# Another order of the routing steps in the last batches, a relu placed between casts, and one drain of GpSimd

## The chip, the cores and the metric

The kernel runs on one core of a Trainium2 chip. TensorE (PE) multiplies matrices and transposes, with its results in PSUM; VectorE (DVE), ScalarE (ACT) and GpSimd (POOL) work on elements; SyncE (SP) issues most DMAs, GpSimd those that gather and scatter rows. Each engine takes its instructions in order. The metric is the device time of one execution in microseconds, as the median of several runs.

## The reference

Attention over 8 batches, 8 heads, 576 positions and 64 dimensions, in which a position sees the blocks of 64 up to its own, and then a mixture of 8 experts that sends each of the 4608 rows to one expert.

```
scores = where(mask, scale * q @ k.T, -1e9)
attn = exp(scores - max) / (sum + 1e-9)
x = (attn @ v).transpose(0, 2, 1, 3).reshape(4608, 512)
logits = x @ w_gate;  e_idx = argmax(logits)
gate_w = softmax(logits)[e_idx];  eom = sigmoid(x @ w_output_gate)
out[rows of e] = gate_w * eom[:, e] * (relu(x[rows] @ w1[e]) @ w2[e])
```

## The kernel before, in words

**Attention.** The 8 batches of 4 pairs of heads are 32 turns p of one pipeline; turn p computes scores and exponentials of pair p, the transposes of pair p-1 and the products with v of pair p-2. `PLAN` (line 310) is the written order of a turn. S0 to S4 are scores of the five row tiles, M0 to M4 their maxima and scalings (VectorE), E0A to E4 the exponentials (ScalarE), F0 to F6 transposes of the exponentials into PSUM, C0 to C6 the ScalarE copies that empty those buffers, V0, V1 and VM the products, X and XM their copies. "E4-" is E4 of the pair before. Between the second pair and the end of the last one, TensorE, VectorE and ScalarE keep this order as written (line 1154). Transposes, logits and other small results share a pool of three PSUM buffers, `ps_t`; scores have two, `ps_s`.

**A batch's finish.** At each "|" of the plan (eight in a turn) `turns()` advances every generator in `later` by one step. Once a batch's last product is done, `finish_batch` (line 508) joins them: `logits` multiplies x by the gate weights in two parts (lge for the last 64 rows, lgb for the others), `keep` copies them out (ke, kb), `turn_logits` and `turn_last` transpose them, `scale_logits` and `scale_last` divide by the softmax sums, `heads` adds over the heads, `choose` finds the expert as a one-hot `oh`, `ranks` and `own` count its place in the expert's list, `slots` gives the address, `shares`, `gather`, `gate` and `weights` give the row's factor, and `scatter` writes rows' numbers and factors to a table in DRAM with five GpSimd DMAs. T(t) and K(t) transpose and store the 128 rows of tile t. A batch's pace says how this is spread: over 32 steps (pace 1, four pairs) for batches 0 to 4, over 16 (pace 2, two pairs) for 5 and 6, and for batch 7 after all pairs with three steps to a turn. `heads` and two products of `choose` run on GpSimd for batches 0 to 5 and on VectorE for 6 and 7 (line 533).

**The end of attention.** After the last pair, `TAIL` runs out the pipeline, and `first_tiles` (line 1162) puts blocks of the first expert step's first layer between the turns of batch 7's finish, at the turns that `play` is given (line 1180). `route_rest` (line 742) then counts rows for each expert with one small matmul (line 688) and, by a chain of small VectorE operations, makes the list of the remaining steps: which weights (`wsel`, `wneed`) and which rows (`rti`) each takes.

**Expert steps.** A step takes 256, 128 or 64 rows of one expert. Rows are gathered by GpSimd, `turn_x` casts them (ScalarE) and subtracts (VectorE) to a high and a low 16-bit part and turns them by a DMA transpose; `stage_h` is the first layer with a relu after each half, `stage_y` the second, whose scaled result GpSimd scatters to the output (line 1057). Weights are fetched as 32-bit and split likewise (line 886). Steps 0 and 1 use the weights of one expert that is chosen early. From there, outside the turns, order on VectorE, ScalarE and GpSimd comes from the framework's scheduler. The last lines hold a branch for lists longer than 22 steps, which isn't taken here (line 1248).

Of the kernel before, what the change touches and what calls it, by code (L numbers as in the profile page):

```python
# [23 lines left out]
SYNC = mybir.DependencyInfo(mybir.DependencyClass.Sync, mybir.DependencyReason.DATA)  # L24
# [3 lines left out]
def block_attention_top1_moe(  # L28
# [11 lines left out]
    nc = tc.nc  # L40
    B, H, S, D = q.shape
# [253 lines left out]
    def constants():  # L295
# [12 lines left out]


    PLAN = """  # L310
        F0 S1 S0 M1 C0 | | E4- F1 C1 F2 M0 C2 E1A E1B E0A S2 E0B | F3 F4 C3 V0 S3 C4 |
        M2 F6 F5 E2A E2B M3 | C5 C6 V1 S4 VM | E3A E3B X M4 | | XM
    """.split()
    OPENING = "S1 S0 M1 M0 E1A E1B E0A E0B | S2 M2 E2A E2B S3 M3 E3A E3B | S4 M4 | | | E4".split()
    later = []
    CP = 1

    def turns():
        for g in list(later):
            if next(g, later) is later:  # L320
                later.remove(g)

    def play(plan, parts, at=()):

        r = 0
        for name in plan:
            if name != "|":
                parts.pop(name, lambda: None)()
                continue
            for i in range(at.count(r)):  # L330
                next(ahead, None)
            r += 1
            turns()
        while plan is TAIL and (later or r <= max(at, default=0)):
            for i in range(at.count(r)):
                next(ahead, None)
            r += 1
            turns()
# [168 lines left out]

    def finish_batch(b, sums, xT, pace):

        for i, fns in enumerate(finish_steps(b, sums, xT, pace)):  # L510
            for fn in fns:
                fn()
            if pace < 3 or i % pace == pace - 1:
                yield

    def finish_steps(b, sums, xT, pace):

# [12 lines left out]
        se = small.tile([P, NT], F32, name="se")  # L530
        sli = small.tile([P, NT], I32, name="sli")
        held = {}
        eng = nc.gpsimd if b < B - 2 else nc.vector

        def bank():
            return ps_t.tile([P, 512], F32, name="ps_t")
# [21 lines left out]
        def turn(t):  # L558
            r = ROWS[t]
            held["r", t] = pm = bank()  # L560
            for g in range(NP):
                nc.tensor.transpose(pm[0:r, P * g:P * g + P], xT[:, g, Q0[t]:Q0[t] + r], ident)

        def store(t):
            r = ROWS[t]
            xn = sb.tile([P, DM], F32, name="xn", bufs=4)
            nc.vector.tensor_tensor(
                xn[0:r].rearrange("p (h d) -> p h d", d=D), held["r", t][0:r].rearrange("p (h d) -> p h d", d=D),
                rec[0:r, t].unsqueeze(2).broadcast_to([r, H, D]), ALU.mult,
            )  # L570
            nc.sync.dma_start(x_d[b * S + Q0[t]:b * S + Q0[t] + r, :], xn[0:r])
# [98 lines left out]
        big, end = (0, 512), (512, S)  # L670
        T, K = (lambda t: lambda: turn(t)), (lambda t: lambda: store(t))
        lge, lgb, ke, kb = (partial(f, *c) for f in (logits, keep) for c in (end, big))
        if pace == 2:
            return [
                [lge, lgb], [ke], [kb, recips], [turn_logits, turn_last], [scale_logits, T(0)], [scale_last, heads, K(0)], [], [choose],
                [], [T(1), ranks], [own, K(1), T(2)], [K(2)], [slots, shares, T(3)], [gather, gate], [K(3), weights, scatter, T(4)], [K(4)],
            ]
        steps = [
            [lge], [ke, lgb], [kb, recips], [turn_logits], [scale_logits], [turn_last], [scale_last], [heads],
            [], [], [T(0)], [K(0)], [], [choose], [], [],  # L680
            [], [T(1), ranks], [own, K(1), T(2)], [K(2)], [T(3), slots], [shares], [K(3)], [],
            [], [], [T(4)], [K(4)], [gather], [gate], [weights, scatter], [],
        ]
        return steps if b < B - 1 else [fns for fns in steps if fns]

    def counts(col, name):
        pc = ps_t.tile([P, 512], F32, name="ps_t")
# [8 lines left out]
    first = const.tile([P, E], F32, name="first")  # L696
# [23 lines left out]
    def sequence(order, i0, used):  # L720
        seq = []
        for i, kind in enumerate(order):
            k = KINDS.index(kind)
            seq.append((BKIND[k] + used[k], KTILES[k], i0 + i))
            width[i0 + i] = KROWS[k] // KTILES[k]
            used[k] += 1
        return seq

    used = [0] * len(KINDS)
    steps = sequence(ORDER, 0, used)  # L730
# [183 lines left out]
    def split_all(fn, b, src):  # L914
        for c in range(4):
            fn(nc.vector, b, src[c], c)
# [35 lines left out]
    def stage_x(st, halves=None):  # L952
        c, n, i = st
        if i not in xs:
            xs[i] = (
                fs.tile([P, KD, n, P], F16, name="xh", padded_shape=[P, KD, 2, P]),
                fs.tile([P, KD, n, P], BF16, name="xl", padded_shape=[P, KD, 2, P]),
            )
        xh, xl = xs[i]
        for h in range(*(halves or (0, n))):  # L960
            other = i == 0 or (h and i > 1)
            px = (ps_t if other else ps_a).tile([P, 512], F32, name="ps_t" if other else "ps_a")
            px = px.rearrange("p (c n) -> p c n", c=KD)
            xv = xg[i % NXG][:, h].rearrange("t (c p) -> t c p", c=KD)
            for cc in range(KD):
                nc.tensor.transpose(px[:, cc, :], xv[:, cc, :], ident)
            act = nc.scalar.copy(xh[:, :, h], px)
            nc.vector.tensor_tensor(xl[:, :, h], px, xh[:, :, h], ALU.subtract)
        return act

    def turn_x(st, act=None):

        c, n, i = st
        xr = fb.tile([P, n, 2, DM], F16, name="xr", padded_shape=[P, 2, 2, DM], bufs=2)
        xt = fb.tile([P, n, 2, KD, P], F16, name="xt", padded_shape=[P, 2, 2, KD, P], bufs=TX + 1)
        for h in range(n):
            xv = xg[i % NXG][:, h]
            xh, xl = (xr[:, h, j] for j in range(2))
            with tc.issue_after(act.ins) if act else nullcontext():
                nc.scalar.copy(xh, xv)  # L980
            nc.vector.tensor_tensor(xl.bitcast(BF16), xv, xh, ALU.subtract)
        turned(xt.rearrange("p h a c n -> p (h a c) n"), xr.rearrange("t h a d -> t (h a d)"))
        xs[i] = xt[:, :, 0].rearrange("p h c n -> p c h n"), xt[:, :, 1].bitcast(BF16).rearrange("p h c n -> p c h n")

    def turned(dst, src):
        with chain():
            chained[0] = nc.sync.dma_start_transpose(dst, src)

    def stage_h(*args, **kw):
        for act in h_steps(*args, **kw):  # L990
            pay()
        return act

    def pay():
        while owed:
            owed.pop()()
# [134 lines left out]
    TAIL = None  # L1131
    for p in range(B * NP):
        b, hp = divmod(p, NP)
        u = p // 2
        h0 = units[u][1]
        if hp == 0:
            sums = small.tile([P, LAST * H + NP], F32, name="sums", bufs=3)
            xT = sb.tile([P, NP, S], F32, name="xT")
# [36 lines left out]
    TAIL = list(PLAN)  # L1175
    advance(TAIL, B * NP, {})
    advance(TAIL, B * NP + 1, {}, (0, 1))
    with tc.manual_schedule(engines={PE}):
        TAIL = []
        play(TAIL, {}, (1, 2, 3, 3, 3))  # L1180
    route_rest()
    for r in ahead:
        pass
# [1 line left out]
    first_ids = read[0].ins  # L1185
    fetch_x(steps[1], (1, 2))
    stage_y(steps[0])
    act = stage_x(steps[1], (1, 2))
    stage_y(steps[1], (0, 1))


# [11 lines left out]
    def split_after(act, fn, src, st):  # L1203

        with tc.issue_after(act.ins):
            split_all(fn, buf(st[2]), src)

    def run(seq, i0):

        n = len(seq)  # L1210
        for i in range(i0, n):
            if i + LI < n:
                fetch_ids(seq[i + LI])
            if i + LX < n:
                fetch_x(seq[i + LX])
            if i + 1 < n:
                fetch_w(seq[i + 1])

            def between(act):
                if i + TX < n:  # L1220
                    turn_x(seq[i + TX], act)
                if i + 1 < n:
                    split_after(act, split_w1, w1f, seq[i + 1])

            act = stage_h(seq[i], between=between)
            if i > i0:
                act = stage_y(seq[i - 1])
            if i + 1 < n:
                split_after(act, split_w2, w2f, seq[i + 1])
        stage_y(seq[n - 1])  # L1230
        pay()
# [6 lines left out]
    for i in range(3 + LX, 2 + LI):  # L1238
        fetch_ids(steps[i])

    turn_x(steps[2], act)
    turn_x(steps[3], act)
    act = stage_h(steps[1], (1, 2))
    split_after(act, split_w1, w1f, steps[2])
    act = stage_y(steps[1], (1, 2))
    split_after(act, split_w2, w2f, steps[2])
    run(steps, 2)
    mv = nc.values_load(more[0:1, 0:1], min_val=0, max_val=NSTEP)  # L1248
    with tc.If(mv > FKIND[1]):
        chained[0] = read[0] = None  # L1250
        for i in range(LI):
            fetch_ids(extra[i])
        for i in range(LX):
            fetch_x(extra[i])
        fetch_w(extra[0])
        split_all(split_w1, buf(extra[0][2]), w1f)
        split_all(split_w2, buf(extra[0][2]), w2f)
        for i in range(TX):
            turn_x(extra[i])
        run(extra, 0)  # L1260
# [30 lines left out]
```

## Time and profile before

| | |
|---|---|
| median of 3 runs | 769.02 us (767.86 to 769.62) |
| the profiled execution | 767.89 us, span 766.0 us |
| busy: TensorE, ScalarE, VectorE, GpSimd | 723.5, 533.0, 522.0, 344.6 us |
| mean granted clock of TensorE | 0.993 |

The span runs from the first to the last instruction. A timeline row gives start, duration, engine, line and operation, and in brackets how long the engine stood idle before it and what it waited for. Attention takes the first 361 us or so, its end and batch 7's finish some 20 more, the expert steps the rest.

### The profile page before, as it was taken

The page shows a single profiled execution, that of the slowest core. Times are in us where ns is not written, and L with a number is a line of the kernel's source. Part 1 is how long each engine was busy: PE and PEld are TensorE (multiplying, and loading weights), DVE is VectorE, ACT ScalarE, POOL GpSimd, SP SyncE. Part 2 cuts the span into 40 slices and gives each one's busy share as a digit, 9 for nine tenths or more (in the row PEclk, how much of TensorE's full clock was granted, in tenths as well). Part 3 has the DMA queues.
Part 4 walks back from the last instruction along what each step waited for, and adds up shares of the span by engine and source line. Part 5 has one row for each costly group of instructions (what it writes and reads, how often), then busy time and mean ns, then how long its engine had stood idle before and what let it go on. Part 6 is the DMA issues. An engine that isn't in the chain of part 4 may idle for free. (4 is left out here: it accounts for less than half of the span.)

```text
span 766.0 us, 18710 instructions
## 1 busy us (share of the span) xinstructions
PE 723.5 (94%) x6898; PEld 511.6 (67%) x6918; DVE 522.0 (68%) x1053; ACT 533.0 (70%) x1193; POOL 344.6 (45%) x486
## 2 busy tenths in 40 slices
PE   5899999999999997999898999999999999999994
PEld 3676766676677765666766759667586675776661
DVE  6666777767776866675827958578586785876530
ACT  4999887888988885976117768577566775865530
POOL 6654647474748576396447423223223344210111
PEclk9999999999999999999999999999999999999998
DMA  8899778969596964852176996899999978723501
GB/s 154 179 202 197 171 156 170 204 121 231 106 224 109 222 139 108 207 169 77 63 263 181 289 302 205 278 290 379 270 324 304 295 225 284 202 54 99 193 29 44
DMA packets 256629, 147.87 MB, mean 193 GB/s; under 512 B 224144, under 2 KB 224208, under 8 KB 256528
## 3 DMA queue, kind: packets, MB, share of 16 engines
q1 hardware_dynamic: 248416, 127.30, 65.8%
q0 software_dynamic: 8112, 19.29, 8.0%
q8 instruction: 56, 0.92, 0.5%
q14 instruction: 45, 0.37, 0.2%
HBM read 126.03 MB, written 19.34 MB: 190 GB/s over the span
## 5 line engine op out<-in xcount | busy, mean ns | idle before, releaser
L1019 PEld LDWEIGHTS <-w1b 128*128 128x128 f16 (+1 forms) x2208 | 176.5, 98 | 22.3 <-DVE w1b L889 1.1
L1019 PE MATMUL ps_s<-xt,w1b 128*128 128x256 f16 (+5 forms) x1920 | 175.1, 253 | 0.3 <-DVE w1b L889 0.3
L422 ACT ACTIVATE pt<-ps_s,nbs 128x512 f32<-128x512 f32 (+4 forms) x282 | 155.8, 576 | 14.9 <-DVE nbs L415 13.1
L1048 PE MATMUL ps_t<-w2b,hh 128*128 128x512 f16 (+1 forms) x540 | 162.2, 379 | 1.7 <-ACT hh L1027 1.7
L889 DVE TENSOR_TENSOR w2b<-w2f,w2b 128x1024 bf16<-128x1024 f32 x80 | 92.9, 1219 | 90.7 <-ACT w2b L887 90.6
L407 DVE TENSOR_REDUCE nmx<-ps_s 128x2 f32<-128x1024 f32 (+1 forms) x125 | 102.8, 822 | 53.5 <-PE ps_s L392 52.6
L1105 ACT COPY pT<-ps_t 128x512 f32<-128x512 f32 (+1 forms) x221 | 112.4, 563 | 22.9 <-PE ps_t L456 22.1
L1057 POOL DMA_INDIRECT out_dram<-ys,ids x38 | 51.6, 1357 | 158.2 <-ACT ys L1056 88.5
L456 PE MATMUL ps_t<-ident,pt 128*128 128x128 f32 x768 | 108.7, 278 | 5.5 <-DVE lh L579 3.0
L1048 PE MATMUL ps_t<-w2b,hl 128*128 128x512 f16 x280 | 106.1, 379 | 1.3 <-DVE hl L1028 0.3
L1056 ACT ACTIVATE ys<-ps_t,ids 128x512 f32<-128x512 f32 (+1 forms) x38 | 26.1, 686 | 110.2 <-PE ps_t L1048 92.3
L1048 PEld LDWEIGHTS <-hh 128*128 128x128 f16 x560 | 54.2, 98 | 63.6 <-ACT hh L1027 1.9
L456 PEld LDWEIGHTS ps_t<-ident,pt 128*128 128x128 f32 x768 | 84.7, 141 | 15.5 <-ACT lgT L556 5.0
L108 POOL TENSOR_TENSOR sp<-nat,sp 128x320 f16<-128x320 f32 x120 | 89.8, 760 | 8.6 <-DVE sp L105 2.7
L889 DVE TENSOR_TENSOR w1b<-w1f,w1b 128x1024 bf16<-128x1024 f32 x80 | 92.8, 1217 | 0.4
L105 POOL CAST sp<-nat 128x320 f16<-128x320 f32 x112 | 48.6, 450 | 82.4 <-ACT pT L1105 77.1
L887 ACT CAST w1b<-w1f 128x1024 f16<-128x1024 f32 x80 | 78.4, 1046 | 2.9 <-DMA w1f<-in_moe_w_dram 2.9
L887 ACT CAST w2b<-w2f 128x1024 f16<-128x1024 f32 x80 | 77.8, 1043 | 1.6 <-DMA w2f<-in_moe_w_dram 1.6
L390 PE MATMUL ps_s<-tr,tr 128*128 128x512 f16 (+1 forms) x250 | 72.1, 305 | 6.8 <-ACT pt L422 6.5
L491 PE MATMUL ps_a<-pT,vb 128*64 128x384 f32 (+2 forms) x256 | 74.0, 412 | 0.0
L491 PE MATMUL ps_a<-pT,va 128*64 128x384 f32 (+2 forms) x256 | 73.9, 412 | 0.0
L391 PE MATMUL ps_s<-sw,tr 128*128 128x512 f16 (+1 forms) x250 | 70.1, 303 | 0.0
(222 smaller groups left out, 1171.5 us busy)
## 6 DMA issues: line engine op xcount, KB each, us to landing
w1f<-in_moe_w_dram SPq DMA_DIRECT2D x80, 512.0 KB
w2f<-in_moe_w_dram SPq DMA_DIRECT2D x80, 512.0 KB
nat<-in_k_dram SPq DMA_DIRECT2D x15, 576.0 KB
nat<-in_q_dram SPq DMA_DIRECT2D x15, 576.0 KB
x_d<-xn SPq DMA_DIRECT2D x32, 256.0 KB
va<-in_v_dram SPq DMA_DIRECT2D x32, 128.0 KB
vb<-in_v_dram SPq DMA_DIRECT2D x32, 128.0 KB
hh<-in_moe_w_dram SPq DMA_DIRECT2D x4, 512.0 KB
```

Source lines behind the costliest of these rows:

```text
L108: last_lo[0] = lo.tensor_tensor(sp[:, sl, 1, :], self.nats[i][:, sl], sp[:, sl, 0, :], ALU.subtract)
L390: nc.tensor.matmul(o, qq, k1[ab][:, 0:n], start=True, stop=False)
L391: nc.tensor.matmul(o, qq, k2[ab][:, 0:n], start=False, stop=False)
L407: nc.vector.tensor_reduce(nmx[t], at[t], AX.X, ALU.max, negate=True)
L422: last_act[0] = nc.scalar.activation(probs[t][:, ab * n:(ab + 1) * n], at[t, ab], AF.Exp, bias=nbs[t][:, ab:ab + 1], scale=SCALE, accum_ou ...
L456: nc.tensor.transpose(held[i][:, P * j:P * j + P], probs[t][:, sl], ident)
L491: nc.tensor.matmul(pa[half, c0:512], vs[a][:, j, :], rows[:, a, j, c0 - P:512 - P], start=(j == 0), stop=(j == 3))
L887: nc.scalar.copy(hi, src)
L889: eng.tensor_tensor(lo[at], src[at], hi[at], ALU.subtract)
L1019: nc.tensor.matmul(ph[:, f4].rearrange("p (h n) -> p h n", n=w), wv[:, cc, f, :], xv[:, cc], start=(k == 0), stop=(k == 3 * KD - 1))
L1048: nc.tensor.matmul(py, hv[:, f, h], wv[:, f, :], start=(k == 0), stop=(k == 3 * KF - 1))
L1105: last_act[0] = nc.scalar.copy(to, of)
```

## The change

The order of finish steps for batches 5, 6 and 7 is another, `heads` and the two products of batch 5 go to VectorE (GpSimd is used at pace 1 only), and two places in the plan, Z0 and Z1, call steps of the finish at pace 2. Batch 7's steps are one to a turn, with more blocks of the first layer between them. At step 1's second half, the casts of step 2's rows come behind the first of the two relus and those of step 3 behind the second, where both stood ahead of the layer. A GpSimd drain that waits for the last relu is added, and the loads of the branch's value stand ahead of the steps.

```diff
     PLAN = """
-        F0 S1 S0 M1 C0 | | E4- F1 C1 F2 M0 C2 E1A E1B E0A S2 E0B | F3 F4 C3 V0 S3 C4 |
+        F0 S1 S0 M1 C0 | | E4- F1 C1 F2 M0 C2 Z0 E1A E1B E0A S2 E0B | F3 F4 C3 V0 Z1 S3 C4 |
         M2 F6 F5 E2A E2B M3 | C5 C6 V1 S4 VM | E3A E3B X M4 | | XM
     """.split()
-                parts.pop(name, lambda: None)()
+                (hooks if name in hooks else parts).pop(name, lambda: None)()
-        eng = nc.gpsimd if b < B - 2 else nc.vector
+        eng = nc.gpsimd if pace == 1 else nc.vector
+        if pace == 3:
+            return [
+                [lge], [ke, lgb], [kb, recips], [turn_logits, turn_last], [scale_logits, scale_last, heads, T(0)], [K(0), choose],
+                [ranks], [own, T(1)], [slots, shares, K(1), T(2)], [gather, K(2), gate, T(3)], [weights, scatter, K(3), T(4)], [K(4)],
+            ]
         if pace == 2:
+            hooks["Z0"] = kb
+            hooks["Z1"] = lambda: [fn() for fn in (turn_logits, scale_logits, turn_last, scale_last)]
             return [
-                [lge, lgb], [ke], [kb, recips], [turn_logits, turn_last], [scale_logits, T(0)], [scale_last, heads, K(0)], [], [choose],
-                [], [T(1), ranks], [own, K(1), T(2)], [K(2)], [slots, shares, T(3)], [gather, gate], [K(3), weights, scatter, T(4)], [K(4)],
+                [lge, lgb], [ke], [recips], [], [heads, T(0)], [K(0), choose], [], [T(1)],
+                [K(1), ranks], [own, T(2)], [K(2), slots, shares], [T(3), gather], [K(3), gate], [T(4), weights], [K(4), scatter], [],
             ]
-        play(TAIL, {}, (1, 2, 3, 3, 3))
+        play(TAIL, {}, (3, 4, 6, 6, 6, 8, 9, 10, 11))
...
-    def run(seq, i0):
+    def run(seq, i0, retire=False):
...
             act = stage_h(seq[i], between=between)
+            if i == n - 1 and retire:
+                tc.add_manual_dep(nc.gpsimd.drain().ins, act.ins.name, SYNC, reason="behind the last first layer")
...
-    turn_x(steps[2], act)
+    act = stage_h(steps[1], (1, 2), between=lambda act: turn_x(steps[2], act))
     turn_x(steps[3], act)
-    act = stage_h(steps[1], (1, 2))
     split_after(act, split_w1, w1f, steps[2])
     act = stage_y(steps[1], (1, 2))
     split_after(act, split_w2, w2f, steps[2])
-    run(steps, 2)
     mv = nc.values_load(more[0:1, 0:1], min_val=0, max_val=NSTEP)
+    run(steps, 2, retire=True)
```

## Rows read from the trace of the kernel before

**Rows 1.** Timeline of TensorE: instructions it waited for (start, us, what, idle before).
```profile
284.12 0.66 PE L456 MATMUL ps_t<-ident,pt 128*128 128x128 f32 x4 [1.48 <-DVE lh L579]
...
293.51 0.19 PE L616 MATMUL ps_a<-oh,below 128*128 128x40 f16 x1 [3.92 <-DVE oh L610]
...
305.69 0.63 PE L456 MATMUL ps_t<-ident,pt 128*128 128x128 f32 x4 [1.05 <-DVE zs L652]
...
334.55 0.65 PE L456 MATMUL ps_t<-ident,pt 128*128 128x128 f32 x4 [1.55 <-DVE lh L579]
...
350.89 2.53 PE L456 MATMUL ps_t<-ident,pt 128*128 128x128 f32 x20 [1.15 <-ACT xT L1105]
...
373.65 0.60 PE L562 MATMUL ps_t<-ident,xT 128*64 128x128 f32 x4 [1.57 <-DVE xn L567]
...
407.63 0.39 PE L1048 MATMUL ps_t<-w2b,hh 128*128 128x512 f16 x1 [1.72 <-ACT hh L1027]
```

**Rows 2.** Busy time by window: PE, PEld, DVE, ACT, POOL, PEclk, DMA share, GB/s.
```profile
234.60:276.09 41.49, 40.68 (x435) 29.20 (x431) 30.73 (x88) 35.91 (x113) 25.46 (x44) 1.00 0.87 169
276.09:326.45 50.36, 42.69 (x439) 30.60 (x437) 31.86 (x97) 36.55 (x113) 29.95 (x46) 0.97 0.60 140
...
295.00:296.00 1.00, 1.00 (x5) 0.51 (x4) 0.94 (x4) 1.00 (x4) 1.00 (x3) 0.50 0.00 0
```

**Rows 3.** Instructions of the kernel's last line: ns min/median/max, first to last start.
```profile
L1286 POOLq DRAIN  x3: 50/109/3825, 761.4 to 765.7; - x3
L1286 SPq DRAIN  x3: 7/7/13, 762.0 to 765.4; - x3
```

**Rows 4.** Groups by line and form, 35 to 350 us: count, busy us, mean ns.
```profile
L407 DVE TENSOR_REDUCE nmx<-ps_s 128x2 f32<-128x1024 f32 x30 | 36.7, 1223 | 32.2 <-PE ps_s L392 32.2
...
L1105 ACT COPY pT<-ps_t 128x512 f32<-128x512 f32 x177 | 100.0, 610 | 22.3 <-PE ps_t L456 21.5 <-issue 0.4
```

**Rows 5.** Timeline of GpSimd: batch 5's adds, and the third-last output scatter.
```profile
289.75 1.45 POOL L598 TENSOR_TENSOR lh<-lh 128x320 f32<-128x320 f32 x2
...
746.15 0.98 POOL L1057 DMA_INDIRECT out_dram<-ys,ids  x1 [9.55 <-ACT ys L1056]
```

**Rows 6.** Timeline of VectorE: batch 6's and 7's finish, a split of weights.
```profile
334.72 1.01 DVE L598 TENSOR_TENSOR lh<-lh 128x320 f32<-128x320 f32 x2
335.76 0.63 DVE L599 TENSOR_TENSOR L<-lh 128x80 f32<-128x80 f32 x1
...
338.55 0.18 DVE L602 TENSOR_REDUCE mx<-L 128x5 f32<-128x40 f32 x1
...
340.18 0.40 DVE L612 TENSOR_TENSOR d<-L,mx 128x40 f32<-128x40 f32 x1
...
365.60 2.13 DVE L598 TENSOR_TENSOR lh<-lh 128x320 f32<-128x320 f32 x2
...
409.03 4.63 DVE L889 TENSOR_TENSOR w1b<-w1f,w1b 128x1024 bf16<-128x1024 f32 x4
```

**Rows 7.** Timeline of TensorE: batch 6's ranks, the routing's count, step 2's start.
```profile
340.08 0.19 PE L616 MATMUL ps_a<-oh,below 128*128 128x40 f16 x1
...
374.31 0.17 PE L688 MATMUL ps_t<-run_cnt,ones 128*128 128x8 f16 x1
...
413.12 7.15 PE L1019 MATMUL ps_s<-xt,w1b 128*128 128x256 f16 x64
```

**Rows 8.** Timeline of ScalarE: casts, weight split, and the last relu.
```profile
404.56 1.95 ACT L980 CAST xr<-xg 128x512 f16<-128x512 f32 x3 [0.62 <-DMA xg<-x_d,ids]
...
407.94 2.94 ACT L887 CAST w1b<-w1f 128x1024 f16<-128x1024 f32 x3
...
739.95 0.60 ACT L1027 ACTIVATE hh<-ps_s 128x512 f16<-128x512 f32 x1 [0.35 <-PE ps_s L1019]
```

**Rows 9.** Instructions of the launch line and of the branch's value, as in rows 3.
```profile
L1275 POOLq DRAIN  x1: 193/193/193, 0.5 to 0.5; - x1
...
L1248 POOLq TENSOR_LOAD <-more x1: 303/303/303, 756.7 to 756.7; - x1
```

More of the change, by code (lines that the diff above doesn't have):

```diff
@@ L314, in block_attention_top1_moe @@
     OPENING = "S1 S0 M1 M0 E1A E1B E0A E0B | S2 M2 E2A E2B S3 M3 E3A E3B | S4 M4 | | | E4".split()
-    later = []
+    later, hooks = [], {}
     CP = 1
@@ L508, in finish_batch @@
     def finish_batch(b, sums, xT, pace):
-        for i, fns in enumerate(finish_steps(b, sums, xT, pace)):
+        for fns in finish_steps(b, sums, xT, pace):
             for fn in fns:
                 fn()
-            if pace < 3 or i % pace == pace - 1:
-                yield
+            yield
     def finish_steps(b, sums, xT, pace):
@@ L672, in finish_steps @@
         lge, lgb, ke, kb = (partial(f, *c) for f in (logits, keep) for c in (end, big))
+        if pace == 3:
[3 more added lines that the diff above has]
+            ]
         if pace == 2:
+            hooks["Z0"] = kb
+            hooks["Z1"] = lambda: [fn() for fn in (turn_logits, scale_logits, turn_last, scale_last)]
             return [
-                [lge, lgb], [ke], [kb, recips], [turn_logits, turn_last], [scale_logits, T(0)], [scale_last, heads, K(0)], [], [choose],
-                [], [T(1), ranks], [own, K(1), T(2)], [K(2)], [slots, shares, T(3)], [gather, gate], [K(3), weights, scatter, T(4)], [K(4)],
+                [lge, lgb], [ke], [recips], [], [heads, T(0)], [K(0), choose], [], [T(1)],
+                [K(1), ranks], [own, T(2)], [K(2), slots, shares], [T(3), gather], [K(3), gate], [T(4), weights], [K(4), scatter], [],
             ]
-        steps = [
+        return [
             [lge], [ke, lgb], [kb, recips], [turn_logits], [scale_logits], [turn_last], [scale_last], [heads],
@@ L683, in finish_steps @@
         ]
-        return steps if b < B - 1 else [fns for fns in steps if fns]
     def counts(col, name):
@@ L1187, in block_attention_top1_moe @@
     stage_y(steps[0])
-    act = stage_x(steps[1], (1, 2))
+    stage_x(steps[1], (1, 2))
     stage_y(steps[1], (0, 1))
```

## The prediction

> **What bounds the kernel now.** I began with the page's busy times and its slices: TensorE is busy 94% of the span and the other engines at most 70%, so the time is TensorE's work plus what it stands idle. Then the timeline of TensorE alone, for the instructions it had to wait for. Past the opening most waits are short, and in the last 340 us there is none worth naming. The large ones that the change touches are in [rows 1]: in the finish of batch 5 (284.12, 293.51, 305.69), of batch 6 (334.55, 350.89), of batch 7 (373.65), and at step 1's second half (407.63). The reader is to see who released each: VectorE's scaled logits or one-hot, a buffer, or ScalarE's relu, never data from DRAM. Third, the table of windows [rows 2]: four pairs of heads take 41.49 us in an undisturbed batch and 50.36 in the stretch of batch 5's finish, 8.87 more, and in one part of it the granted clock is 0.50, the lower of the two levels (1.2 GHz), after the 3.92 us in which TensorE stood still. Fourth, the end: the last GpSimd DMA is followed by a drain of GpSimd that lasts 3.8 us, on which the rest waits [rows 3].
>
> So time can come from three places: the waits of rows 1, the clock behind the longest of them, and the drain. A saved wait shifts everything behind it, since TensorE has no slack later.
>
> **The change part by part.**
>
> *Batch 5, first wait (1.48).* TensorE's transposes F5 waited for a PSUM buffer that the scaled logits free; VectorE had these behind the 1.22 us maximum M3 [rows 4]. Now logits are kept after C2 and scaled before S3 and M2. Wait gone. Price: turn_last wants a buffer that C3 frees, because only three exist: from the order on ScalarE some 0.25 us (0 to 0.6), right ahead of S3.
>
> *Batch 5, second wait (3.92).* GpSimd's queue made the head sums late (1.45 us for two adds, begun at 289.75 [rows 5]) and the ranks' matmul waited for the one-hot. Now VectorE adds them. For batch 6 it does already: 1.01 and 0.63 us [rows 6].
>
> *What is late next.* heads, the store K0 and choose now all stand ahead of M4 on VectorE, whose order is as written here; choose used to come behind M4. And M4 feeds E4, ScalarE copies C1 only behind E4, and C1 frees the buffer for the second pair's F2. From M3's start: M3 and its scaling 1.5 (the scaling an estimate of 0.3), heads 1.65, K0 0.7 (estimated like C1), choose 2.0 (338.55 to 340.58), M4 with its scaling 1.0 (estimated below M3, being narrower), E4 0.75 (estimated a little above C1), C1 0.6: 8.2 us [rows 4, 6]. M3 now begins some 0.65 us after F5, since the scaled logits and M2 go first. TensorE needs from F5 to F2 the 5.53 us from 334.55 to 340.08 [rows 1, 7] (T1, which now comes ahead of F0, is in it), plus ranks 0.2, T2 0.45 and F1 0.45 (four transposes of the 20 that took 2.53 us [rows 1] are 0.5): 6.6. So it waits 8.2 + 0.65 - 6.6 = 2.25, with turn_last 2.5, and I add 0.2 for sums rounded: 2.7 us in each of batches 5 and 6.
>
> *Batch 5, third wait (1.05).* It ended with the weights' instruction on VectorE; T4 and K3 now come on with slots and gather done two turns earlier. Gone.
>
> *Sum for batch 5.* Waits 6.45; of the other 2.42 of the 8.87, I count 1.5 as lost to the half clock (a mean of 0.97 over 50.36 us) and the rest as another pair's own. Recoverable 7.95, less 2.7, less 0.4 (estimated, 0 to 1.4) because two swaps of a later unit's keys, each about K0's length, stand in VectorE's queue in the same pair: 4.9 gained. Below, it could be 1.5 (chain longer); above, 8.
>
> *Batch 6.* Old waits 1.55 + 1.15 = 2.7; new 2.7: 0, between -2.5 and +2.7.
>
> *Batch 7 and the relu, taken together.* The 1.57 us wait (T4 for the buffer of a store) goes: first-layer blocks now lie between the turns, and the steps of each turn are shorter. The 1.72 us wait goes too: ScalarE ran four casts of later rows, three of them behind the gather (0.62 us wait, 404.56 to 406.51 [rows 8]), ahead of the relu; now the first relu goes first, so that TensorE can begin the second layer on the first half, and the second relu needs only two casts ahead of it. But what is late next is the weight split for step 2. Its high parts follow the relu and the casts on ScalarE (407.94), its low parts follow on VectorE until 413.66 [rows 6, 8], and the first block of the step's first layer needs all four. Moved: second relu at about 405.2 (the gather's rows still land at 404.5), two casts to 407.1, low parts 408.15 to 412.8. The first block then ends at 413.0, where it now ends at 413.12 + 1.3 = 414.4 (12 of the 64 matmuls that take 7.15 us [rows 7]): 1.4 us kept of 3.3. What is queued behind the relu is the same either way. One thing goes against it: the count matmul for the rest of the routing now runs at 374.31 [rows 7], in the hole beside T4. The change fills that hole with first-layer blocks. If the count comes behind all of them (about 376.6), the weights' and rows' fetches start 1.3 us later, and only 0.1 is kept. If the shorter chain lets it slip in earlier, up to 3.3 is kept. I take 1.4.
>
> *The register loads.* Each engine loads the branch's value ahead of the steps rather than at the end. GpSimd's took 0.3 us at its last DMA [rows 9]: 0.3 gained. The load that now comes in TensorE's queue I cost at nothing, because matmuls wait in line ahead of it; without that cover it is another 0.3 lost.
>
> *The drain.* At the start, with no DMA of its own outstanding, GpSimd's drain took 0.193 us; at the end the first of three took 3.825, the two behind it 0.109 and 0.050 [rows 3, 9]. So most of its length is something done once and not again. Placed behind the last relu (ends 740.55 [rows 8]) it has until GpSimd's next DMA at 746.15 [rows 5]: 5.6 us of cover for 3.8. Behind it stand only the three last stores of y; without cover they'd be 3.8 us late, but the last has 10 more us. At the end SyncE reaches its own drain at 762.0, while GpSimd's now ends at 765.2 [rows 3]; with GpSimd's short, the rest waits for SyncE: 765.2 - 762.05 = 3.15 gained. Lower bound 0, upper 3.8, its whole length.
>
> The Trainium skill ("VectorE: DVE Perf Modes", "The DRAIN you can't avoid") says that the drains of a kernel's preamble and postamble take some 12 ns on all five engines. By that rule nothing could be gained and this term would be 0. The 3.825 us row differs, and the measurement decides.
>
> Sum against the profiled execution (span 766.0, whole 767.89): 4.9 + 0 + 1.4 + 0.3 + 3.15 = 9.75, so 758.1. The median of the three runs, 769.02, lies 1.13 above that execution; against it, **759.2**.
>
> **The rivals.**
>
> *A. The drain at the end stays long* (0.22). It may wait for something that follows any DMA, and three DMAs come after the new drain; or it lands elsewhere in GpSimd's queue, so that the change doesn't do what it says. For: those two short ones follow with no DMA between. Against: the start's 0.193. Time: 759.2 + 3.15 = 762.4.
>
> *B. Slower: VectorE's adds wait out GpSimd's* (0.05). Three adds in heads and five small products in choose read two SBUF tensors each, on an engine whose neighbour runs casts and subtractions almost without a break in these pairs. If each of the eight waits out one GpSimd operation of 0.73 us [rows 5], M4 is 5.8 us later, TensorE waits 8.5 us per batch, and, being over 3.92, loses another 1.5 each to the clock. Batch 5: 7.95 - 8.5 - 1.5 - 0.4 = -2.5; batch 6: 2.7 - 10 = -7.3; with 4.85 from the rest, 5 us slower: 774. It decides the sign from 3.4 us per batch on (2 x 3.4 + 3 for the clock = 9.75). For: batch 7's two adds took 2.13 us beside a running GpSimd, not 1.01 [rows 6]. Against: that is 1.1 in two adds, and choose's chain ran in 2.0 with GpSimd busy.
> The Trainium skill ("SBUF — State Buffer", "SBUF: two separate sides") has the rule: the port pair that both share is an exclusive lock for a whole instruction. The 2.13 agrees with that.
>
> *C. The chain is somewhat longer and the count comes last* (0.13): 1.7 us more in both batches (1.1 in the adds as in batch 7, 0.6 in the products) and 1.3 at the relu: 759.2 + 4.7 = 763.9.
>
> *D. TensorE's waits hardly reappear* (0.10), because buffers fall otherwise than I laid them out: 7.95 + 2.7 + 3.3 + 3.45 = 17.4, so 751.6.
>
> **How the numbers follow.** Forecast 0.50, with a range of its own of 756 to 762. A change under 0.2% can't be told from none here, so faster means below 767.5. The forecast, A and D are faster; of C's 0.13 I put 0.05 where both its delays double (768.6) and the time stays within 0.2%, and B's 0.05 is slower: 0.90, 0.05, 0.05. The 8-in-10 range takes in A and C and the nearer half of D: 753.5 to 765.
>
> **What would show it.** Right: no wait over 1 us before an F5 or before the ranks; one of 1 to 2 us before F2 in the second pairs, released by ScalarE's copy or a store; the four-pair stretch from 50.4 to about 45.5, at full clock; TensorE waiting for w1b, not for the relu, near 400 us; a long drain of GpSimd near 735 us and a short last one, SyncE's drain then being the late one. Wrong: waits over 3 us and the lower clock in pairs of batches 5 or 6; a last drain still over 3 us; a start of step 2 not earlier than the batches' gain.

## The result, and the profile after

The changed kernel took 760.85 us (median of four runs, 759.22 to 763.15) beside 769.12 for the kernel before: a ratio of 0.9895, 95% interval 0.9866 to 0.9923. Run again beside the last experiments, six times, it took 763.21 beside 769.12, 0.9924 (0.9899 to 0.9949). The change is faster by 6 to 8 us; the forecast was 759.2, a gain of 9.8. The profiled execution fell from 767.89 to 760.33 us, its span from 766.0 to 758.4, so 7.6 us have to be found. This is one of the faster of the changed kernel's ten executions (759.22 to 765.41), so 7.6 lies near the top of what the change gains.

The timeline of TensorE in the kernel after, the instructions it waited for (columns as in [rows 1]):

```profile
288.21 0.66 PE L456 MATMUL ps_t<-ident,pt 128*128 128x128 f32 x4 [1.34 <-DVE xn L566]
290.24 0.19 PE L615 MATMUL ps_a<-oh,below 128*128 128x40 f16 x1 [0.59 <-DVE oh L609]
292.81 0.66 PE L456 MATMUL ps_t<-ident,pt 128*128 128x128 f32 x4 [1.33 <-ACT pT L1110]
...
303.24 1.09 PE L456 MATMUL ps_t<-ident,pt 128*128 128x128 f32 x8 [0.26 <-DVE xn L566]
307.85 0.38 PE L390 MATMUL ps_s<-tr,tr 128*128 128x512 f16 x1 [0.88 <-ACT pt L422]
311.88 0.41 PE L399 MATMUL ps_s<-tr,tr 128*64 128x512 f16 x2 [0.92 <-ACT pt L422]
...
339.82 0.66 PE L456 MATMUL ps_t<-ident,pt 128*128 128x128 f32 x4 [1.57 <-ACT pT L1110]
...
373.90 0.17 PE L693 MATMUL ps_t<-run_cnt,ones 128*128 128x8 f16 x1
...
408.03 1.03 PE L1024 MATMUL ps_s<-xt,w1b 128*128 128x256 f16 x8 [1.76 <-DMA xt<-xr]
409.52 0.61 PE L1024 MATMUL ps_s<-xt,w1b 128*128 128x256 f16 x4 [0.45 <-DVE w1b L894]
410.66 9.56 PE L1024 MATMUL ps_s<-xt,w1b 128*128 128x256 f16 x86 [0.53 <-DVE w1b L894]
```

The 1.48, 3.92, 1.05, 1.57 and 1.72 us of [rows 1] are gone. In their place the reader sees three waits in batch 5's second pair (1.34 in front of F0, for the store K0; 0.59 in front of the ranks; 1.33 in front of F2, for ScalarE's copy), one of 0.26, one of 1.57 in batch 6 in front of F2, and at step 2 a first wait of this part that comes from a DMA: the transposed rows xt, then the split weights. The 0.88 and 0.92 stand where the kernel before had one wait that is not in [rows 1]:

```profile
311.89 0.38 PE L390 MATMUL ps_s<-tr,tr 128*128 128x512 f16 x1 [1.22 <-ACT pt L422]
```

The windows of the kernel after that answer to [rows 2] (an undisturbed four pairs, and the four of batch 5's finish):

```profile
234.10:275.99 41.89, 41.08 (x441) 29.46 (x438) 30.72 (x88) 36.15 (x113) 25.63 (x44) 1.00 0.88 169
275.99:323.92 47.93, 42.16 (x438) 29.73 (x436) 35.62 (x102) 36.09 (x113) 28.31 (x42) 1.00 0.66 151
```

50.36 became 47.93, at full clock (0.97 before).

The end, by line (L1232 is the new drain, L1253 the register loads, L1255 the branch, and INC_SWDGE_SEM an instruction that GpSimd runs just ahead of its last drains), answering to [rows 3] and [rows 9]:

```profile
L1232 POOLq DRAIN  x1: 3580/3580/3580, 736.9 to 736.9; - x1
...
L1253 POOLq TENSOR_LOAD <-more x1: 307/307/307, 753.0 to 753.0; - x1
...
L1255 POOLq INC_SWDGE_SEM  x1: 254/254/254, 756.5 to 756.5; - x1
...
L1292 POOLq DRAIN  x3: 50/109/300, 756.8 to 758.1; - x3
L1292 SPq DRAIN  x3: 7/7/13, 757.5 to 757.8; - x3
```

From the last matmul's end to the span's end it was 10.54 us before (755.46 to 766.0) and is 6.62 now (751.78 to 758.4): 3.92. That and 3.68 by which the last matmul ends earlier make the 7.6. The 3.68 come apart at the matmuls of L490, which begin each pair's product with v, V0 (L490 has this number in both kernels): from the second pair of batch 5's stretch to the same pair one batch on, 2.42 us less (50.36 to 47.94: 279.83 to 330.19, now 279.73 to 327.67); to batch 7's last pair 0.07 less; from there to step 2's first layer 2.49 less (54.83 to 52.34); and from that to the end 1.41 more (342.34 to 343.75). 0.10 is the start of the stretch.

### The profile page after: what moved, and what is told of

It reads as the page before. It is cut to its first block, busy times and chain, and to the rows that moved or that the text cites. A ratio compares the mean times of both kernels' runs of the same rounds, so it can differ in the third digit from the quotient of the medians.

```text
span 758.4 us, 18741 instructions
## 1 busy us (share of the span) xinstructions
PE 724.5 (96%) x6918; PEld 510.5 (67%) x6918; DVE 525.5 (69%) x1058; ACT 532.1 (70%) x1193; POOL 341.5 (45%) x481
## 4 chain that ended last, share of the span: by engine, by line
PE 69%; DVE 10%; DMA 7%; ACT 7%; issue 4%; POOL 2%; POOLq 1%; SPq 0%; DVEq 0%; ACTq 0%
PE ps_s L1024 23%; PE ps_t L1053 19%; PE ps_t L456 7%; PE ps_a L491 5%; ACT pt L422 4%; DMA tr<-sp 4%; PE ps_s L390 3%; PE ps_s L391 3%; POOL tab_d L658 2%; PE ps_t L499 1%; PE ps_t L561 1%; ACT pT L1110 1%; DVE nmx L407 1%; PE ps_s L399 1%; PE ps_a L1077 1%
## 5 line engine op out<-in xcount | busy, mean ns | idle before, releaser
L1053 PE MATMUL ps_t<-w2b,hh 128*128 128x512 f16 (+1 forms) x560 | 166.9, 379 | 0.0
L1062 POOL DMA_INDIRECT out_dram<-ys,ids x38 | 48.9, 1288 | 155.2 <-ACT ys L1061 87.7
```

The lines of the kernel that those rows point to most:

```text
L1053: nc.tensor.matmul(py, hv[:, f, h], wv[:, f, :], start=(k == 0), stop=(k == 3 * KF - 1))
```

## The experiments

Twelve more kernels ran, the changed one again among them, on three chips; medians compare only within one. On the first, the kernel before took 769.41 us.

**The change without its drain, and the drain alone.**

```
 run(steps, 2, retire=True)   ->   run(steps, 2)            # changed kernel, without
 kernel before + drain behind the last relu                 # alone
```

> The changed kernel without its drain of GpSimd behind the last first layer; all else as changed. Theory (the drain at the end costs by how much GpSimd has issued since its last drain, and an early one takes that length under the last steps' work): the drain at the end is long again, 3.6 to 3.9 us instead of 0.30, the stretch from the last matmul's end to the span's end is 10.3 to 10.6 us instead of 6.6, and the time is 3.6 to 4.0 us above the changed kernel's 760.85, so 764.4 to 764.9. Rival (the end is short because the work before it is ordered otherwise, and the drain adds nothing): 760.5 to 761.2, with a drain at the end of 0.3 to 1 us.

> The kernel before with the drain alone. Theory: the last matmul ends where it did, the tail behind it falls from 10.5 to 6.6 us, and the time falls by 3.6 to 4.0 us, to 765.1 to 765.5. Rival (the drain's length is spent on the path of the last output rows, because their scatters are queued behind it on GpSimd): a gain below 2 us, with the last scatters issued later against the last matmul than before.

Without: 765.51, ratio 0.9967 (0.9946 to 0.9988). Alone: 764.99, ratio 0.9957 (0.9938 to 0.9976). The rows of GpSimd at the end, without the drain:

```profile
L1255 POOLq INC_SWDGE_SEM  x1: 1115/1115/1115, 758.1 to 758.1; - x1
...
L1292 POOLq DRAIN  x3: 50/109/3825, 759.2 to 763.6; - x3
```

and with the drain alone:

```profile
L1288 POOLq DRAIN  x3: 50/109/300, 761.4 to 762.6; - x3
```

From the last matmul's end to the span's end it is 10.26 us without the drain (753.64 to 763.9) and 6.37 with the drain alone (756.53 to 762.9). The theory holds in both, the rivals fall: by the traces the drain is worth 3.6 us with the new order and 4.2 without it. All traces agree: 10.1 to 10.7 us in the four kernels without the drain, 6.3 to 6.8 in the ten with it. On GpSimd itself the last drain fell by 3.5 us, and INC_SWDGE_SEM ahead of it, which the forecast did not hold, from 1.115 to 0.254 us as well; not all of this shows at the end, where SyncE's drain is then the late one.

The kernel without the drain also says what the rest of the change is worth: 2.5 us by the ratio (0.9 to 4.2). In its profiled execution the last matmul ended 1.5 us earlier than before, counted from the start of batch 5's stretch, and not 3.6 as in the changed kernel, which runs the same work up to there. At step 2 it waits about as long as the changed kernel (2.9 and 2.7 us), but behind these waits its granted clock falls to the lower level, 0.50, for some 3.4 us:

```profile
410.00:415.00 5.00, 4.52 (x27) 3.17 (x28) 5.00 (x6) 3.77 (x4) 4.39 (x3) 0.66 0.50 160
```

**What sets a drain's length.**

```
-            if i == n - 1 and retire:
+            if i in (2, 10, n - 1) and retire:
```

> The changed kernel with two more drains of GpSimd, behind the first layers of steps 2 and 10 (about 67 and 90 of its 143 DMAs issued by then), to read their lengths. Theory (a drain's length grows with the DMAs that GpSimd has issued since its last one; 143 gave 3.825 us at the end of the kernel before, about 140 gave 3.58 and 3 more 0.30): about 1.5 to 1.9 us at the first, 0.5 to 0.8 at the second, 1.1 to 1.5 at the third, 0.3 at the end. Rival (the first drain of a program is dear whatever went before): 3.5 us or more at the first, 0.3 us or less at each of the others.

One execution, 773.70 us on the second chip. The three drains of that line, one by one:

```profile
L1232 POOLq DRAIN  x1: 6137/6137/6137, 433.1 to 433.1; - x1
...
L1232 POOLq DRAIN  x1: 7059/7059/7059, 566.4 to 566.4; - x1
...
L1232 POOLq DRAIN  x1: 2834/2834/2834, 750.5 to 750.5; - x1
```

Both were wrong: the first came after 74 DMAs of GpSimd, and the second, after 32 more, was the longest; the third, after 35 more, took 2.83. A drain in the middle of the steps may also wait for transfers still under way: the mean busy share of the DMA engines was 0.97 and 0.93 during the first two and 0.01 during the third. No run tests that. That a drain just ahead leaves the last one short, 0.30 behind three DMAs, all kernels with the drain show; what sets the length stays open.

**Batch 5: the engine or the order.**

```
-        eng = nc.gpsimd if b < B - 2 else nc.vector      # kernel before
+        eng = nc.gpsimd if b < B - 3 else nc.vector      # engine alone
-        eng = nc.gpsimd if pace == 1 else nc.vector      # changed kernel
+        eng = nc.gpsimd if b < B - 2 else nc.vector      # order alone
```

> The kernel before, with the head sums and products of batch 5 on VectorE instead of GpSimd and the order of its finish untouched. Theory (the order matters as well as the engine): the wait of 3.92 us in front of the ranks goes down to 0 to 0.6 us and the half clock behind it goes, but the waits of 1.48 and 1.05 us stay, and V0 of batch 6 comes 3.5 to 5 us earlier: 764 to 765.6. If VectorE's products beside GpSimd's tree additions are what made the changed chain 1.6 us longer than I reckoned, heads and choose take 4.5 to 5.5 us here too. Rival (the new order does the work, the engine is minor): a gain below 1.5 us, 767.6 or more.

> The changed kernel with the head sums and products of batch 5 back on GpSimd; the new order of its steps stays. Theory (the engine is all that counts in batch 5: in the run with the engine alone the probability matmuls of the first pair behind it, at L490, came 2.72 us earlier against the kernel before, with the new order 2.42): the wait in front of the ranks is 3 to 4 us again, the first L490 of the pair that started at 330.19 before is back to 72.5 to 74 us behind the matmul of S1 near 257, and the time is 2 to 3.5 us above the changed kernel, 763 to 764.4. Rival (the order alone hides the 1.48 and 1.05 us waits): within 1 us of the changed kernel, 761 to 762.

The engine alone: 768.51, ratio 0.9998 (0.9977 to 1.0019), no gain in time, where I expected 764 to 765.6. But the L490 stretch, 50.36 us before and 47.94 changed, is 47.64 (278.71 to 326.35): the engine gives all that batch 5 gained, 2.72, though the waits of 1.48 and 1.05 us stay, and then it is lost further on: step 2's first layer begins 57.9 us behind batch 7's last pair, beside 54.83, after a wait for the relu and with the clock at the lower level behind it (0.66 is the mean of 5 us). Two of its waits in batch 5, the one at step 1 and the window there:

```profile
289.68 0.19 PE L616 MATMUL ps_a<-oh,below 128*128 128x40 f16 x1 [1.21 <-DVE oh L610]
293.96 0.66 PE L456 MATMUL ps_t<-ident,pt 128*128 128x128 f32 x4 [1.43 <-DVE xn L567]
...
405.73 0.61 PE L1048 MATMUL ps_t<-w2b,hh 128*128 128x512 f16 x1 [2.21 <-ACT hh L1027]
...
405.00:410.00 5.00, 4.05 (x12) 1.61 (x14) 4.49 (x6) 4.93 (x7) 4.39 (x5) 0.66 1.09 190
```

The order alone ran on the second chip, where all kernels took longer (the kernel before 777.27): ratio 1.0010 (0.9982 to 1.0038). Its stretch was 52.52 us (285.51 to 338.03) beside 49.31 to 49.43 in the three other kernels run there, which have it with VectorE; its ranks waited 1.88 us, less than the 3 to 4 that I expected. So in batch 5 it is the engine that counts, and the new order is worth nothing that these runs show. The time that I expected was against the changed kernel, which has none on that chip.

VectorE's head sums say why the chain was longer than I had reckoned. Here are those of the kernel after, in batch 5, 6 and 7, and of the engine-alone kernel in batch 5:

```profile
284.74 2.28 DVE L597 TENSOR_TENSOR lh<-lh 128x320 f32<-128x320 f32 x2
287.05 0.51 DVE L598 TENSOR_TENSOR L<-lh 128x80 f32<-128x80 f32 x1
...
332.82 1.39 DVE L597 TENSOR_TENSOR lh<-lh 128x320 f32<-128x320 f32 x2
...
363.00 0.95 DVE L597 TENSOR_TENSOR lh<-lh 128x320 f32<-128x320 f32 x2
```

```profile
283.16 2.82 DVE L598 TENSOR_TENSOR lh<-lh 128x320 f32<-128x320 f32 x2
```

The same two adds (of 128x320 and 128x160; a row shows the form of its first) cost 0.95, 1.39, 2.28 and 2.82 us. Beside the first and the last of these rows GpSimd subtracts two 128x320 tiles, for 1.5 us; in batch 6 it works on 128x256 tiles, and in batch 7 it is done 0.24 us after the adds begin. On the second chip the same adds of batch 5 happened to begin when that pair of subtractions was over, and took 1.24 us. GpSimd in the kernel after, then GpSimd and VectorE in the kernel with three drains:

```profile
284.74 1.54 POOL L108 TENSOR_TENSOR sp<-nat,sp 128x320 f16<-128x320 f32 x2
```

```profile
287.58 1.53 POOL L108 TENSOR_TENSOR sp<-nat,sp 128x320 f16<-128x320 f32 x2
...
289.63 1.24 DVE L597 TENSOR_TENSOR lh<-lh 128x320 f32<-128x320 f32 x2
```

No run took GpSimd's work away on purpose, so that its subtractions are the cause is read from these contrasts, not shown by an experiment.

**The relu.**

```
-    act = stage_h(steps[1], (1, 2), between=lambda act: turn_x(steps[2], act))
-    turn_x(steps[3], act)
+    turn_x(steps[2], act)
+    turn_x(steps[3], act)
+    act = stage_h(steps[1], (1, 2))          # changed kernel, without; alone: the reverse, in the kernel before
```

> The kernel before with relu of step 1's second half issued between the casts of step 2's rows, nothing else. Theory: the wait of 1.70 us in front of step 1's second layer (half 2) goes, TensorE reaches step 2's first layer 1.7 us earlier, and finds there its rows or its weight split late by about as much, since both follow the route and not TensorE: a gain of 0 to 0.6 us, 768.5 to 769.1. Rival (casts and split come earlier too): the gain is the whole 1.7 us, 767.4.

> The changed kernel with relu of step 1's second half back behind the casts of the next rows. Theory (the earlier batches' gain is only passed on if relu does not wait for the rows: with the engine of batch 5 alone, 2.6 us of it were lost in front of step 1's second layer, and relu alone gained nothing): a wait of 4 to 6 us in front of step 1's second layer, TensorE at half clock behind it, and a time 2.5 to 5 us above the changed kernel, 763.5 to 766 against 761. Rival (relu is worth its own 0.3 to 1 us, as I had put it): 761.3 to 762.

Relu alone: 768.14, ratio 0.9992 (0.9973 to 1.0012), so anything from 0.9 us lost to 2.1 us gained. Its 1.72 us wait went, and step 2's first layer began 1.7 us sooner behind batch 7's last pair (53.09 us against 54.83). It did not find its rows or weights late there, as I had expected: its one wait was short,

```profile
412.88 7.29 PE L1019 MATMUL ps_s<-xt,w1b 128*128 128x256 f16 x64 [0.27 <-ACT w1b L887]
```

and from batch 7's last pair to the last matmul 1.5 us of the 1.7 were kept. The rival is nearer to this trace than the theory. That the whole span is as long as before comes from batch 6 of that execution, which lies ahead of the edit and ran 1.1 us longer. The change without it, on the third chip (the kernel before 769.12): 764.60, ratio 0.9946 (0.9927 to 0.9966), 1.4 us above the changed kernel there, with intervals that overlap. Its row and the window behind:

```profile
406.59 0.61 PE L1053 MATMUL ps_t<-w2b,hh 128*128 128x512 f16 x1 [5.96 <-ACT hh L1032]
```

```profile
400.00:405.00 5.00, 0.63 (x12) 0.46 (x9) 1.58 (x3) 2.01 (x4) 3.56 (x4) 0.83 0.79 261
405.00:410.00 5.00, 3.19 (x8) 1.17 (x10) 4.49 (x6) 5.00 (x8) 3.36 (x3) 0.50 0.91 219
```

TensorE reaches step 1's second layer 5.3 us earlier than before (its wait begins at 400.64 beside 405.92) and stands 5.96 us behind the casts of rows, the last of which ends only 1.0 us earlier (405.47 beside 406.51), and the clock falls to the lower level. Its last matmul then ends 0.5 us later than before, counted in both from a matmul near 257 us. All of its gain is the drain's, as in the kernel with the drain alone (0.9957). The theory holds in this trace; the time rose less than I expected, 1.4 instead of 2.5 to 5.

**Batch 7 in the old order.** The list of its steps and its three-step turns as before, `play(TAIL, {}, (1, 2, 3, 3, 3))`.

> The changed kernel with batch 7's finish in the order of before (sums first, then two transposes, two additions and so on, three steps to a turn, and the old places of the first expert tiles). Theory (batch 7's order and relu add up: each alone moves TensorE to a wait of the other's): the 1.57 us wait at the second row tile is back, the last row gather before step 2 goes out 1 to 2 us later, step 2's first layer starts 1.5 to 3 us later and the time is 1 to 3 us above the changed kernel, 762 to 764. Rival (batch 7's order is worthless, because the count runs as late as before): 760.5 to 761.3.

776.44 on the second chip, ratio 1.0003 (0.9980 to 1.0025). Step 2's first layer came 54.66 us after batch 7's last pair, beside 54.38 in the kernel with three drains, which has the new order up to there. The changed kernel itself has no time on that chip, so the worth of batch 7's order is not settled: 0.3 us by the trace.

**Step 2's start: the count, the indices, the weights.**

```
+  [slots, count, shares, ...]            # count: counts(B, "cnt1") called here, used by route_rest
-    fetch_w(steps[2], first_ids)
     fetch_ids(steps[2])
+    fetch_w(steps[2], read[0].ins)       # weights behind the indices of step 2
```

> The changed kernel with the count of the experts' tokens (one matmul, one copy) issued in batch 7's finish behind the slots, instead of behind all of it and the next rows' turn. Theory (step 2's start waits for the chain count, route, indices, gather, rows' transposes and weight splits): the copy of the count runs at 370 to 371.5 instead of 376.0 us, the table of slots is out 3 to 5 us earlier, the rows of step 2 are gathered 1.5 to 3 us earlier, and of the waits of 1.76, 0.46 and 0.53 us at step 2's start at most 1 us stays: 758.3 to 759.4. Rival (the weights of step 2, 4 MB, and the earlier scatters and gathers of GpSimd's queue set it): a gain under 0.5 us, 760.4 to 761.

> The changed kernel once more, on the chip of the three runs below, as their base and to narrow its median: on a chip where the kernel before takes 769 us, 760 to 762; on one where it takes 777, 768 to 772, if the gain is the same there. If it gains less there (rival: the waits that the change fills are filled otherwise on that chip), 773 to 776.

> The changed kernel with the 4 MB of weights of step 2 let go only when the row indices of step 2 are in, instead of those of step 1's second half. Theory (step 2's start waits for its row indices, which land 3.8 to 6.2 us after their issue beside the weights against 1.7 us without them; the weights themselves are not awaited): the gather of step 2's rows goes out 1.5 to 3 us earlier against the second gather of step 1, the rows' casts 1 to 2.5 us earlier, and the waits of 1.76, 0.46 and 0.53 us in front of step 2 shrink by 1 to 2.5 us: 758.5 to 760 where the changed kernel takes 761. Rival (the weights come to be the late ones, 4 us later than now): the waits for the weight splits grow and the time is 0.5 to 2 us above the changed kernel.

> The same with the count moved ahead as well. Theory (the early route was worth nothing in its own run because the indices then landed beside the weights all the same, 4.7 us after their last issue): now the indices go out 2 us earlier and land in under 2 us; the gather of step 2's rows is 3 to 4 us earlier than in the changed kernel, its waits in front of step 2 are gone, and the time is 2 to 3 us below it, 758 to 759 against 761. Rival (the scatters of the slots set the chain, not the route): no faster than the run with the indices first alone.

Count early, second chip: 775.76, ratio 0.9987 (0.9963 to 1.0011). The routing's indices were ready 2.6 us earlier than in the three-drains kernel there, and the row gather for step 2 went out at the same time (121.82 and 121.77 us behind the L490 that begins batch 5's stretch): its index read landed beside the weights. On the third chip the changed kernel took 763.21, above the 760 to 762 that I expected; with the indices first 766.98, ratio 0.9968 (0.9951 to 0.9985), slower by 3.8; with the early count as well 760.79, ratio 0.9899 (0.9866 to 0.9932). GpSimd's last index read and the gather behind it, in the kernel after:

```profile
390.72 0.56 POOL L853 DMA_DIRECT2D ids<-tab_d  x1 [0.49 <-issue]
394.78 1.06 POOL L864 DMA_INDIRECT xg<-x_d,ids  x1 [3.50 <-DMA ids<-tab_d]
```

With the indices first, GpSimd, then SyncE's transposes, then TensorE:

```profile
391.30 0.56 POOL L853 DMA_DIRECT2D ids<-tab_d  x1 [0.49 <-issue]
392.16 1.07 POOL L864 DMA_INDIRECT xg<-x_d,ids  x1 [0.30 <-issue]
```

```profile
402.65 10.68 SPq L992 DMA_TRANSPOSE xt<-xr  x2
```

```profile
414.12 6.11 PE L1024 MATMUL ps_s<-xt,w1b 128*128 128x256 f16 x34 [7.24 <-ACT w2b L892]
```

The 3.50 us wait for the indices is gone, as expected, and the casts of the rows began 1.9 us sooner. But the weights now leave 3.6 us later (391.12 and 386.57, each counted from a matmul near 257 us), and are under way when the rows are transposed by DMA: the two transposes took 10.68 us in SyncE's queue instead of 4.67, and TensorE waited 7.24 us at step 2. The row names ScalarE's cast of w2b as what ended this wait, but that cast ended at 414.12, and the load of the weights for this very matmul had begun at 414.09, so the cast did not end it; the transposes, for which this matmul waits too, left SyncE's queue at 413.33:

```profile
414.09 0.99 PEld L1024 LDWEIGHTS <-w1b 128*128 128x128 f16 x6 [7.71 <-ACT w2b L892]
```

My rival saw a loss from late weights, but put it on the weights' splits; the place is the transposes. With the early count as well the weights leave 1.5 us later than in the changed kernel, and the transposes take 7.13. The changed kernel's median is 2.4 us above that, but the intervals overlap, and in the profiled executions the early count's last matmul is the later one by 1.4 us: whether it beats the change isn't settled.

## Why the prediction was right, and where its terms were not

The sum was 9.75, the profile has 7.6. The time came inside the range because the parts that the drain and batch 5's engine carry did what was said; three terms were mis-sized, and one assumption failed. That the sum is not further off is in part luck: the drain gave 0.8 more than its term, where batch 5 gave 2.5 less. The second median, 763.21, lies outside the forecast's own 756 to 762 and inside the wide range.

- *Batch 5, old waits gone*: right, all three of [rows 1], and the half clock.
- *Batch 5, sum 4.9*: 2.42 measured. The lost clock was put at 1.5; TensorE's busy time in the stretch fell by 0.53 only (42.69 to 42.16). New waits were put at 2.7 + 0.4; the waits over 0.25 us are 1.34 + 0.59 + 1.33 + 0.26, and the later pair's 1.22 became 0.88 + 0.92: 4.1, and 4.6 with the shorter ones (5.8 us of waits in the stretch instead of 7.7). The 1.33 in front of F2 is a wait that was forecast; the 1.34 in front of F0 is not: the store K0, which frees its buffer, stands behind the long sums on VectorE. The chain's sums were sized by batch 6's 1.01 and 0.63 [rows 6]; with its neighbour busier they took 2.8, and choose 2.5 instead of 2.0. That is rival C's first part, at about the size I gave it (1.7), in batch 5 alone. Rival B's price, that each of eight operations waits out one of GpSimd's, did not come: waits over 3.92 there are none. But its mechanism fits the first add, which is longer by about what two of GpSimd's subtractions last beside it.
- *Batch 6, 0*: right (0.07; 0.5 in the second profile of the changed kernel): its 1.55 and 1.15 went, and waits of 0.42, 0.36 and 1.57 came.
- *Batch 7 and the relu, 1.4*: 2.49 at step 2's start, 1.08 after step 2's waits (2.9 and 0.5 in the second profile, and 2.8 and a loss of 1.1 in that of the kernel without the drain, where the clock fell).
- The step that failed is the sentence that a saved wait shifts everything behind it, since TensorE has no slack later. Step 2's first layer began 5.1 us earlier than before, but what follows the routing moved less: the count ran at 373.90, where it ran at 374.31 [rows 7], and the gather at 394.78, where it was 396.40. With relu behind the casts of these rows TensorE waits there for most of what it has gained, and then loses more at the lower clock: the engine alone 0.9998, the change without relu no more than its drain. So the batches' gain needs the relu. The other way round nothing is shown: relu alone kept 1.5 us in its trace, and its times can't tell that from none. The two together, which the sum added up as separate terms, ended the last matmul between 1.5 and 3.6 us earlier in the three profiles that have both; the sum had 6.3 for them.
- *What is late next*: partly right. The split weights were late (0.45 and 0.53), but ahead of them came the rows' transposes, a DMA that the sum did not hold (1.76).
- *Register loads, 0.3*: 0. They stand ahead of the steps in the program, but GpSimd's ran at 753.0, at its last DMA (753.2) as before, TensorE's and ScalarE's near the end too (747.7 and 751.9); SyncE's ran early (381.8).
- *The drain, 3.15*: 3.9. SyncE's drain, which bounds this gain, itself came 0.8 us sooner behind the last matmul (5.7 us instead of 6.5), as INC_SWDGE_SEM on GpSimd shrank by 0.9. The long drain ran at 736.9, ahead of the DMA at 742.47, and the last one took 0.30. Rival A is out. SyncE's drain is the late one at the end, as said.

## What to carry to other kernels

Ask of each saved wait where the next meeting point with a chain that does not move is: a gain ahead of it counts only as far as the work at that point is free of the chain, and an edit that is worth nothing alone may be worth something once another takes the meeting point away. A lower clock behind the wait can cost as much as the wait. Size an operation by a row with the same neighbour at work, not by the same operation elsewhere. A cost at the program's very end, such as a drain's, can be taken out almost whole by doing it earlier beside other work.

## What the runs showed of the hardware

- A drain of GpSimd took 3.58 and 3.83 us after its 141 and 144 DMAs, 0.30 after three more, and 6.1 and 7.1 us in the middle of the steps.
- Two adds on VectorE (128x320 and 128x160) took 0.95 to 2.82 us, the longest beside GpSimd's subtractions of 128x320.
- Two DMA transposes of rows took 4.67, 7.13 and 10.68 us, the longer the later the 4 MB of weights had been let go (1.5 and 3.6 us later).
- Behind waits of TensorE at the end of step 1 or at step 2 the granted clock fell to the lower level, 0.50, in some executions and not in others with waits about as long (2.9 us in all at step 2 with the fall, 2.7 without).
- One chip of three ran the kernel before 8 us slower, with waits of TensorE for nothing that the trace names (0.4 to 1.4 us in nearly every batch); on it the three kernels with most of the change that ran more than once came out level with the kernel before. Why is open.
